# Top-k attention and an MLP: how many heads of a unit VectorE turns, and the order of the last batch

## The chip, the cores and the metric

The kernel runs on one core of a Trainium2 chip. The metric is the device time of one execution in microseconds (us). An execution uses five engines side by side: TensorE (PE in the profile; its weight loads are PEld), VectorE (DVE), ScalarE (ACT), GpSimd (POOL), and SyncE (SP), which here only issues DMAs. Each engine takes its instructions in the order in which the program was written, and waits for others by semaphores.

## The reference

Two blocks follow each other, in float32. Attention has 8 batches, 8 heads, 576 rows and 64 columns per head; of each row of scores only the 32 largest count:

```python
scores = scale * np.matmul(q, k.transpose(0, 1, 3, 2))
kth = np.partition(scores, -top_k, axis=-1)[..., -top_k:-top_k + 1]
scores = np.where(scores >= kth, scores, -1000000000.0)
attn = np.exp(scores - np.max(scores, axis=-1, keepdims=True))
attn = attn / (np.sum(attn, axis=-1, keepdims=True) + 1e-09)
x = np.matmul(attn, v)          # then (B,H,S,D) -> (B, S, H*D)
```

The MLP works on the rows of x (8 x 576 rows of 512):

```python
xn = (x - mu) / np.sqrt(var + 1e-06) * g_ln
out = x + np.maximum(xn @ w_ch1, 0.0) @ w_ch2     # 512 -> 2048 -> 512
```

The weights arrive as float64 and are converted on the chip, during the first batch.

## The kernel before, in words

**Units, groups and jobs.** The heads are taken in pairs, A and B. The 576 query rows of a pair are four tiles of 128 rows and a rest of 64. A *unit* is one tile for both heads (both heads' rests together fill one tile of 128). A *group* is some units of one head pair, a *job* has one group here. `parts` (L731 to L739) lists the groups of a batch: in batch 0 tiles 0 and 1, tiles 2 and 3, and the rest, each for all four head pairs; in batch 1 tiles 0 and 1, then 2, 3 and the rest; in batches 2 to 6 tiles 0, 1 and the rest, then 2 and 3. Batch 7 has the rest first, alone, for the four pairs, then tiles 0 and 1, then 2 and 3. That makes 160 units, 20 a batch.

**What a unit goes through.** `scores` (L329) multiplies on TensorE and copies to `sc` on ScalarE. `halve` (L363) and `select` (L381) find the 32nd largest score: VectorE takes maxima of eight and strikes them out (L391, L399, L386), GpSimd helps with two integer operations (L376, L379). `mask` and `weigh` on ScalarE (L426, L436) turn the scores into exponentials `e`, with their sums. Then `e` has to be turned, so that the keys lie on the partitions, as `pt`. There are two ways:

- `turn` (L481): TensorE transposes four blocks of 128 x 128 per head into PSUM (L490), and ScalarE copies them to `pt` (L502). A last block holds the last 64 keys of both heads (L519, L520); it always goes this way. Units of the rest always go this way too (L497, L510 to L513).
- `move` (L462): VectorE transposes 32 x 32 blocks within each head (L468, one instruction for a head), into the space of the unit's own scores; a DMA stores that to `turned` in device memory (L473) and four DMAs bring it back, each block to its partitions (L476). SP issues them.

`u.moved` (L763, L764) says which way: from batch 2 on, a unit is moved, with both heads, unless it is a rest or the last of its group. `values` (L539) then multiplies a group's `pt` with v on TensorE (L544, L551); `place` and `place_rest` turn the result back and scale it by the sums into `x`, the input of the MLP. The rest rows of two successive batches share one tile of x, `r`, so there is a rest tile for every second batch.

**Steps and the order written out by hand.** The loop from L894 runs over steps n. In step n VectorE selects unit n and halves unit n+1; TensorE makes the scores of unit n+2; unit n-1 is masked and unit n-2 weighed and turned or, at the step's end, moved; a group whose last unit is n-3 is multiplied with v. (The first units run one step closer.) All engines' instructions are written in this one order.

**The MLP as filling.** When the tiles of x of a job round are due, `give` (L847) adds a `Block` of them to the list `todo`: transposes of x (L648), hidden products (L664; 64 products, each as wide as the block has rows) and projections (L680; 16 products of 512 columns for each tile). Blocks have 2 tiles, or 3 with a rest tile (in batch 7: a block of 1, for the rest alone). The dictionary `gives` (L777 to L797) sets their steps. `fill` stands at eight places of a step and takes pieces off the list as long as their cost, in constants of the planner (0.44 a transposed tile, 0.0017 a row of a product), fits the pace that `slot` (L857) sets. Up to step 17 the pace is the difference of `dve_cost` and `pe_cost`; after it, `slot` divides what is left, less a reserve of 4.0, evenly over the steps to the next gifts, and takes the smallest such pace over all later gifts:

```python
for m in sorted(gives):
    if m > n:
        even = min(even, (left - RESERVE) / (m - n))
        left += sum(b.cost() for b in gives[m])
```

After the last gift (step 163) the whole list is taken without regard to VectorE. A tile of x is turned only a step after its rows were centred (`centred`, L622), and the list is taken strictly in order.

Of the kernel before, what the change touches and what calls it, by code (L numbers as in the profile page):

```python
# [21 lines left out]
J = 4  # L22
# [7 lines left out]
def kernel(  # L30
# [41 lines left out]
    nc = tc.nc  # L72
    P = nc.NUM_PARTITIONS
    B, H, S, D = q.shape
# [3 lines left out]
    JP = J * P  # L78
# [43 lines left out]
    def turned():  # L122
        return brief("tp")
# [18 lines left out]
    class Piece:  # L142
# [10 lines left out]
        def __init__(self, i):  # L153
            self.i = i
            if i < NF:
                self.c, self.nb = i % NC, i // NC
                n0 = self.nb * DM
                self.src = w_ch1[self.c * P : (self.c + 1) * P, 2 * n0 : 2 * (n0 + DM)]
                self.dst = w1[:, self.c, n0 : n0 + DM]
            else:  # L160
                f = i - NF
                self.src = w_ch2[f * P : (f + 1) * P, :]
                self.dst = w2[:, f, :]
# [146 lines left out]
    class Unit:  # L310
        def __init__(self, job, group, qt):
            self.job, self.group, self.qt = job, group, qt
            self.rest = qt == J
            self.tiles = [(0, 1)] if self.rest else [(0,), (1,)]

            self.moved = False
            self.e = None
            self.weighed = 0

# [130 lines left out]
    def place_of(u):  # L450

        g = u.group
        if g.pt is None:
            g.pt = ptpool.tile([P, 2 * J + 1, GQ], FP32, tag="pt", name="pt")
            g.blocks = g.pt[:, 0 : 2 * J].rearrange("p c n -> p (c n)").rearrange(
                "p (i h c n) -> p h i c n", h=2, c=J, n=32
            )
        return sum(P for x in g.qts if x < u.qt) // 32  # L460

    def move(u):  # L462

        i0 = place_of(u)
        ni = P // 32
        blocks = u.sc[:].rearrange("p t n -> p (t n)")[:, 0 : 2 * JP]
        for t in range(2):
            nc.vector.transpose(  # L468
                blocks.rearrange("p (j t c n) -> p j t c n", j=ni, t=2, c=J)[:, :, t],
                u.e[:, t, t * R : t * R + JP].rearrange("p (c j k) -> p j c k", c=J, k=32),  # L470
            )
        hbm = hbmpool.tile([P, 2 * JP], FP32, tag="turned", name="turned")
        nc.sync.dma_start(hbm[:], blocks)  # L473
        for j in range(ni):
            to = u.group.pt[j * 32 : (j + 1) * 32, 0 : 2 * J].rearrange("k c n -> k (c n)")
            nc.sync.dma_start(  # L476
                to[:, i0 * 2 * P : (i0 + ni) * 2 * P].rearrange("k (i x) -> k i x", i=ni),
                hbm[:, j * 2 * P : (j + 1) * 2 * P].rearrange("(i k) x -> k i x", k=32),
            )

    def turn(u):  # L481

        g = u.group
        i0 = place_of(u)
        q0 = i0 * 32

        def part(t):
            ps = turned()
            for c in range(J):
                nc.tensor.transpose(  # L490
                    ps[:, c * P : (c + 1) * P], u.e[:, t, c * P + t * R : (c + 1) * P + t * R],
                    ident[:],
                )
            if u.rest:
                both = ps[:].rearrange("p (c h n) -> p h c n", h=2, n=R)
                for h in range(2):
                    nc.scalar.copy(  # L497
                        g.blocks[:, h, i0 : i0 + R // 32],
                        both[:, h].rearrange("p c (i n) -> p i c n", n=32),
                    )  # L500
            else:
                nc.scalar.copy(  # L502
                    g.blocks[:, t, i0 : i0 + P // 32],
                    ps[:].rearrange("p (c i n) -> p i c n", c=J, n=32),
                )

        def last():
            ps = turned()
            if u.rest:
                nc.tensor.transpose(ps[0:R, 0:P], u.e[:, 0, JP:S], ident[:])  # L510
                nc.tensor.transpose(ps[:, P : 2 * P], u.e[:, 0, JP - R : S], ident[:])
                for h in range(2):
                    nc.scalar.copy(  # L513
                        g.pt[h * R : (h + 1) * R, 2 * J, q0 : q0 + R],
                        ps[h * R : (h + 1) * R, h * (P + R) : h * (P + R) + R],
                    )
            else:
                ends = u.e[:].rearrange("p t n -> p (t n)")[:, JP : JP + P]
                nc.tensor.transpose(ps[:, 0:P], ends, ident[:])  # L519
                nc.scalar.copy(g.pt[:, 2 * J, q0 : q0 + P], ps[:, 0:P])  # L520

        heads = () if u.moved else range(len(u.tiles))
        return [lambda t=t: part(t) for t in heads] + [last]

    xs, xps, rs, oTr, dr = {}, {}, {}, {}, {}
# [13 lines left out]
    def values(g):  # L539
        vb = g.job.v  # L540
        av = brief("av")
        for c in range(J):
            for h in range(2):
                nc.tensor.matmul(  # L544
                    av[h * D : (h + 1) * D, 0 : g.nq],
                    vb[:, h * J + c, :],
                    g.blocks[:, h, 0 : g.nq // 32, c, :],
                    start=(c == 0),
                    stop=False,
                )  # L550
        nc.tensor.matmul(  # L551
            av[:, 0 : g.nq], g.job.ends[:], g.pt[:, 2 * J, 0 : g.nq],
            start=False, stop=True,
        )
        g.oT = otpool.tile([P, GQ], FP32, tag="oT", name="oT")
        nc.scalar.copy(g.oT[:, 0 : g.nq], av[:, 0 : g.nq])  # L556
# [173 lines left out]
    for b in range(B):  # L730
        parts = [[0, 1], [2, 3], [J]]  # L731
        if b:
            parts = [[0, 1], [2, 3]]
            if b == B - 1:
                parts = [[J]] + parts
            else:
                parts[b < 2].append(J)
        for qts in parts:
            jobs += [Job(b, hp, [qts]) for hp in range(NHP)]  # L739
    units = []  # L740
# [20 lines left out]
    EARLY = jobs[NHP].first  # L761

    for u in units[jobs[5 * NHP].first :]:  # L763
        u.moved = not u.rest and u is not u.group.units[-1]  # L764


    full = slice(0, P)
# [9 lines left out]
    for j in jobs:  # L777
        if j.hp == NHP - 1:
            b = j.b
# [23 lines left out]
    def at(i):  # L803
        return units[i] if 0 <= i < N else None

    def after(n):

        turned = at(n - 1) if n - 1 < EARLY else at(n - 2) if n - 2 >= EARLY else None
        last = at(n - 2) if n - 2 < EARLY else at(n - 3) if n - 3 >= EARLY else None
        return turned, last.group if last and last is last.group.units[-1] else None  # L810

    def due(n):

        ahead = [n + 1] if n < CONVERTING else [n + 2]
        if n == CONVERTING:
            ahead = [n + 1, n + 2]
        return [units[i] for i in ahead if i < N]

    DVE_UNIT, DVE_REST, DVE_MOVE, DVE_TURN = 8.6, 5.0, 1.4, 1.45


    turns = {}
# [5 lines left out]
    def pe_cost(n):  # L828
        c = 0.0
        for x in due(n):  # L830
            c += 1.25 if x.rest else 1.5
        ex, g = after(n)
        if ex:
            c += 0.67 if ex.rest else 0.15 if ex.moved else 1.0
        if g:
            c += 0.6 + 7.8e-3 * g.nq
        return c

    def dve_cost(n):
        u, ex = at(n), after(n)[0]  # L840
        c = 4.0 if u is None else DVE_REST if u.rest else DVE_UNIT
        if n <= CONVERTING:
            c += 1.0
        c += DVE_TURN * (n in turns) + 0.85 * sum(b.n for b in gives.get(n, []))
        return c + DVE_MOVE if ex and ex.moved else c

    def give(n):  # L847
        early = not all(map(done, ready))
# [8 lines left out]
    def slot(n):  # L857


        if n <= CONVERTING:  # L860
            return max(0.0, dve_cost(n) - pe_cost(n)) / SLOTS
        left = sum(t[1] for t in todo)
        if n > last_give:
            even = left / max(1, END - 1 - n)
        else:
            even = 99.0
# [4 lines that stand above are left out]
        return max(0.0, even) / SLOTS  # L871
# [22 lines left out]
    for n in range(END):  # L894
# [4 lines left out]
        u, nxt, mk = at(n), at(n + 1), at(n - 1)  # L899
        ex, g = after(n)  # L900
# [3 lines left out]
        parts = turn(ex) if ex else []  # L904
# [1 line left out]
        last = ex and ex is ex.group.units[-1]  # L906
        quick = ex.group if last and ex.group.quick else None

        moved = ex is not None and ex.moved
        sent, stores[:] = stores[:], []  # L910

        if ex and not early:
# [21 lines left out]
        fill()  # L934
        if g:
            values(g)
        if parts and not moved:
            parts[0]()
        if ex and ex.rest:
            keep_den(ex)  # L940
# [58 lines left out]
        if moved:  # L999
            move(ex)  # L1000
# [46 lines left out]
```

## Time and profile before

Four executions took 1664.87 to 1668.89 us, with a median of 1666.33. The profiled one took 1668.89 us, its span from the first to the last instruction 1667.1 us, and the mean granted clock of TensorE was 0.981.

| | busy us | share of the span |
|---|---|---|
| TensorE | 1562.9 | 94% |
| TensorE's weight loads, beside it | 939.8 | 56% |
| VectorE | 1469.1 | 88% |
| ScalarE | 1041.7 | 62% |
| GpSimd | 672.3 | 40% |

Some groups of instructions: projection products L680 544.9 us, hidden products L664 552.0, VectorE's maxima L399 490.8 and strikes L386 391.9 and 125.9, its transposes in `move` L468 89.4 (136 of them), TensorE's transposes of e L490 96.5 (608), ScalarE's copies of them L502 69.8 (120).

In the lines of the profile an instruction group reads: line, engine, operation, what it writes and reads, shapes, count, busy us, mean ns of one, idle time of its engine just before, and who ended that idle time. A timeline row has the start, the length from there to the end of the merged instructions, engine, line, operation and count, and in brackets the idle time before it and who ended it. One float32 product appears as two records, one transpose as one. The ends of matmuls are modelled, so what a product costs is read from start to start.

### The profile page before, as it was taken

The page shows a single profiled execution, that of the slowest core. Times are in us where ns is not written, and L with a number is a line of the kernel's source. Part 1 is how long each engine was busy: PE and PEld are TensorE (multiplying, and loading weights), DVE is VectorE, ACT ScalarE, POOL GpSimd, SP SyncE. Part 2 cuts the span into 40 slices and gives each one's busy share as a digit, 9 for nine tenths or more (in the row PEclk, how much of TensorE's full clock was granted, in tenths as well). Part 3 has the DMA queues.
Part 4 walks back from the last instruction along what each step waited for, and adds up shares of the span by engine and source line. Part 5 has one row for each costly group of instructions (what it writes and reads, how often), then busy time and mean ns, then how long its engine had stood idle before and what let it go on. Part 6 is the DMA issues. An engine that isn't in the chain of part 4 may idle for free.

```text
span 1667.1 us, 24932 instructions
## 1 busy us (share of the span) xinstructions
PE 1562.9 (94%) x7057; PEld 939.8 (56%) x7057; DVE 1469.1 (88%) x4611; ACT 1041.7 (62%) x2615; POOL 672.3 (40%) x881
## 2 busy tenths in 40 slices
PE   2668899989899999999999999999999999999998
PEld 1336457556355475745547575745547575756764
DVE  5997999999999999999999999999879895988600
ACT  6886877767656666666656665656555565666620
POOL 5776763343443433343243433443243423333110
PEclk9878999999999999999999999999999999999999
DMA  7423333001433335233443335324333241222200
GB/s 176 88 81 92 95 62 61 22 14 22 100 107 88 99 82 135 91 91 89 108 120 95 86 103 127 97 71 99 99 96 99 72 114 48 60 78 69 81 13 13
DMA packets 303185, 139.30 MB, mean 84 GB/s; under 512 B 250820, under 2 KB 285640, under 8 KB 303048
## 3 DMA queue, kind: packets, MB, share of 16 engines
q1 hardware_dynamic: 298312, 137.12, 31.2%
q10 hardware_dynamic: 4736, 0.59, 0.3%
q8 instruction: 57, 0.93, 0.2%
q14 instruction: 80, 0.66, 0.1%
HBM read 92.54 MB, written 45.09 MB: 83 GB/s over the span
## 4 chain that ended last, share of the span: by engine, by line
PE 65%; DVE 23%; ACT 4%; issue 4%; POOL 3%; DMA 1%; SPq 0%; ACTq 0%; POOLq 0%; DVEq 0%
PE hps L664 23%; PE ops L680 22%; PE scps L354 7%; DVE m L399 7%; PE av L544 6%; DVE hi L386 6%; DVE hi L391 3%; DVE lo L386 2%; PE tp L490 2%; PE av L551 2%; DVE hi L375 2%; DVE size L193 1%; ACT sc L335 1%; POOL lo L376 1%; ACT e L426 1%
## 5 line engine op out<-in xcount | busy, mean ns | idle before, releaser
L664 PE MATMUL hps<-xT,w 128*128 128x256 f32 (+2 forms) x2176 | 552.0, 397 | 4.9 <-ACT xT L653 4.9
L680 PE MATMUL ops<-w,h 128*128 128x512 f32 x1152 | 544.9, 600 | 0.0
L399 DVE MAX8 m<-hi 128x8 f32<-128x304 f32 x1152 | 490.8, 464 | 3.3
L664 PEld LDWEIGHTS hps<-xT,w 128*128 128x128 f32 x2176 | 388.0, 191 | 110.0 <-issue 30.6
L376 POOL TENSOR_TENSOR lo<-sc,hi 128x576 int32<-128x576 int32 (+1 forms) x160 | 208.6, 1304 | 488.8 <-DVE hi L375 254.2
L386 DVE MATCH_REPLACE8 hi<-m,hi 128x304 f32<-128x304 f32 x864 | 391.9, 462 | 0.0
L680 PEld LDWEIGHTS ops<-w,h 128*128 128x128 f32 x1152 | 200.6, 191 | 185.9 <-issue 181.8
L391 DVE MAX8 hi<-lo 128x8 f32<-128x288 f32 x576 | 235.2, 446 | 38.3 <-POOL lo L379 37.2
L354 PE MATMUL scps<-kT,qT 64*128 64x288 f32 (+3 forms) x1344 | 222.1, 430 | 37.7 <-DVE qT L306 27.3
L335 ACT COPY sc<-scps 128x288 f32<-128x288 f32 x576 | 199.6, 408 | 70.2 <-PE scps L354 49.3
L426 ACT ACTIVATE e<-sc,m 128x576 f32<-128x576 f32 x288 | 224.1, 778 | 10.2 <-DVE m L399 7.1
L436 ACT ACTIVATE e<-e,bias 128x576 f32<-128x576 f32 x288 | 224.7, 780 | 0.7
L379 POOL TENSOR_TENSOR lo<-lo,sc 128x576 int32<-128x576 int32 (+1 forms) x160 | 207.2, 1295 | 12.5
L354 PEld LDWEIGHTS scps<-kT,qT 64*128 64x128 f32 (+1 forms) x1344 | 122.9, 179 | 154.0 <-issue 57.6
L544 PE MATMUL av<-pt,vb 128*64 128x256 f32 (+2 forms) x1152 | 148.3, 400 | 0.2 <-ACT pt L513 0.2
L675 ACT ACTIVATE h<-hps 128x512 f32<-128x512 f32 (+1 forms) x156 | 88.4, 567 | 87.1 <-PE hps L664 85.8
L375 DVE TENSOR_TENSOR hi<-sc 128x576 f32<-128x576 f32 (+1 forms) x160 | 115.3, 721 | 25.7 <-ACT sc L335 25.7
L386 DVE MATCH_REPLACE8 lo<-hi,lo 128x288 f32<-128x288 f32 x288 | 125.9, 445 | 0.0
L693 POOL TENSOR_TENSOR o<-o,x 128x512 f32<-128x512 f32 x32 | 42.0, 1313 | 207.3 <-ACT o L689 207.3
L556 ACT COPY oT<-av 128x256 f32<-128x256 f32 (+2 forms) x72 | 26.8, 373 | 157.7 <-PE av L551 157.7
L490 PE MATMUL tp<-ident,e 128*128 128x128 f32 x608 | 96.5, 283 | 27.9 <-ACT e L436 27.3
L544 PEld LDWEIGHTS av<-pt,vb 128*64 128x64 f32 x1152 | 75.9, 142 | 78.2 <-ACT e L436 15.1
(70 smaller groups left out, 1264.3 us busy)
## 6 DMA issues: line engine op xcount, KB each, us to landing
turned<-sc SPq DMA_DIRECT2D x68, 512.0 KB, 2.6
pt<-turned SPq DMA_DIRECT2D x272, 128.0 KB, 3.0
vb<-in_v_dram SPq DMA_DIRECT2D x144, 128.0 KB, 2.7
raw<-in_moe_w_ch_dram SPq DMA_DIRECT2D x32, 512.0 KB, 4.3
kin<-in_k_dram SPq DMA_DIRECT2D x128, 72.0 KB, 2.7
qin<-in_q_dram SPq DMA_DIRECT2D x120, 72.0 KB, 2.7
out_dram<-o SPq DMA_DIRECT2D x32, 256.0 KB, 2.1
ends<-in_v_dram SPq DMA_DIRECT2D x144, 16.0 KB, 2.3
```

Of the source, the lines that this page charges most:

```text
L335: nc.scalar.copy(u.sc[:, t, s * HALF : (s + 1) * HALF], made[s][t][:, 0:HALF])
L354: nc.tensor.matmul(ps[i * R : i * R + ql, o : o + width], qT[r, q0 : q0 + ql], kT[r, k0 : k0 + width], start=True, stop=True,)
L376: nc.gpsimd.tensor_tensor(lo.bitcast(I32), a.bitcast(I32), hi.bitcast(I32), ALU.subtract)
L379: nc.gpsimd.tensor_tensor(lo.bitcast(I32), lo.bitcast(I32), b.bitcast(I32), ALU.add)
L386: nc.vector.match_replace(x[:, t], m[:, t, :], x[:, t], LOWEST)
L391: nc.vector.max(u.hi[:, t, o : o + 8], u.lo[:, t])
L399: nc.vector.max(m[:, t, :], u.hi[:, t])
L426: nc.scalar.activation(u.e[:, t], u.sc[:, t], AF.Prelu, bias=u.thr[:, t, 7:8], scale=-1.0, alpha=SLOPE)
L436: nc.scalar.activation(u.e[:, t], u.e[:, t], AF.Exp, bias=u.bias[:, t : t + 1], scale=-scale / SLOPE, accum_out=g.den[:, col : col + 1],)
L544: nc.tensor.matmul(av[h * D : (h + 1) * D, 0 : g.nq], vb[:, h * J + c, :], g.blocks[:, h, 0 : g.nq // 32, c, :], start=(c == 0), stop=False,)
L664: nc.tensor.matmul(ps["h"][:, o : o + N], w1[:, c, f * P : (f + 1) * P], xT[0][:, c, 0:N], start=(c == 0), stop=(c == NC - 1),)
L680: nc.tensor.matmul(ps[i][:], hT[f][:, i * P : (i + 1) * P], w2[:, f, :], start=(f == 0), stop=(f == NF - 1),)
```

## The change

A unit's `moved` becomes a number of heads: 0, 1 or 2. From batch 2 to batch 4 the units that were moved with both heads have head B alone turned by VectorE and returned by DMA, and head A by TensorE and ScalarE; from batch 5 on they have both moved, as before. `move` works on the heads from `2 - nt` on and sends half as many bytes for one head. Batch 7 has the same groups as batches 2 to 6, so that its rest units come third in their groups, its rest tile goes into a block of three with tiles 0 and 1, and three of its five units of a head pair are moved rather than two. The planner's constants follow the number of heads.

```diff
-            self.moved = False
+            self.moved = 0
...
-        blocks = u.sc[:].rearrange("p t n -> p (t n)")[:, 0 : 2 * JP]
-        for t in range(2):
+        nt = u.moved
+        blocks = u.sc[:].rearrange("p t n -> p (t n)")[:, 0 : nt * JP]
+        for i, t in enumerate(range(2 - nt, 2)):
             nc.vector.transpose(
-                blocks.rearrange("p (j t c n) -> p j t c n", j=ni, t=2, c=J)[:, :, t],
+                blocks.rearrange("p (j t c n) -> p j t c n", j=ni, t=nt, c=J)[:, :, i],
                 u.e[:, t, t * R : t * R + JP].rearrange("p (c j k) -> p j c k", c=J, k=32),
             )
         hbm = hbmpool.tile([P, 2 * JP], FP32, tag="turned", name="turned")
-        nc.sync.dma_start(hbm[:], blocks)
+        nc.sync.dma_start(hbm[:, 0 : nt * JP], blocks)
         for j in range(ni):
             to = u.group.pt[j * 32 : (j + 1) * 32, 0 : 2 * J].rearrange("k c n -> k (c n)")
+            to = to.rearrange("k (i x) -> k i x", x=2 * P)[:, i0 : i0 + ni, (2 - nt) * P :]
             nc.sync.dma_start(
-                to[:, i0 * 2 * P : (i0 + ni) * 2 * P].rearrange("k (i x) -> k i x", i=ni),
-                hbm[:, j * 2 * P : (j + 1) * 2 * P].rearrange("(i k) x -> k i x", k=32),
+                to, hbm[:, j * nt * P : (j + 1) * nt * P].rearrange("(i k) x -> k i x", k=32)
             )
...
-        heads = () if u.moved else range(len(u.tiles))
+        heads = range(len(u.tiles) - u.moved)
...
-            if b == B - 1:
-                parts = [[J]] + parts
-            else:
-                parts[b < 2].append(J)
+            parts[b < 2].append(J)
...
-        u.moved = not u.rest and u is not u.group.units[-1]
+        if not u.rest and u is not u.group.units[-1]:
+            u.moved = 2 if u.job.b >= B - 3 else 1
...
-    DVE_UNIT, DVE_REST, DVE_MOVE, DVE_TURN = 8.6, 5.0, 1.4, 1.45
+    DVE_UNIT, DVE_REST, DVE_MOVE, DVE_TURN = 8.6, 5.0, 0.7, 1.45
...
-            c += 0.67 if ex.rest else 0.15 if ex.moved else 1.0
+            c += 0.67 if ex.rest else 1.0 - 0.44 * ex.moved
...
-        return c + DVE_MOVE if ex and ex.moved else c
+        return c + DVE_MOVE * ex.moved if ex else c
...
-        moved = ex is not None and ex.moved
+        moved = ex is not None and ex.moved > 0
...
-        if parts and not moved:
+        if len(parts) > 1:
             parts[0]()
```

## The prediction

> **What bounds the kernel now.** I read the page's busy lines and slices first, then the busy time by batch, then single rows of TensorE's timeline to see whether a busy TensorE is a working one.
>
> ```profile
> PE 1562.9 (94%) x7057; PEld 939.8 (56%) x7057; DVE 1469.1 (88%) x4611; ACT 1041.7 (62%) x2615; POOL 672.3 (40%) x881
> PE   2668899989899999999999999999999999999998
> DVE  5997999999999999999999999999879895988600
> ```
>
> TensorE (PE) is idle mainly in the first ten slices, where batches 0 and 1 run and the weights are converted; VectorE (DVE) is full from there to slice 28, then has gaps. Who ends last has to be read by batch. The halving on VectorE runs once per unit; its 41st, 61st, 81st, 101st, 121st and 141st starts, at 408.7, 592.7, 777.0, 962.6, 1149.8 and 1357.7 us, cut the span into batches 2 to 7. Busy time of the engines in these stretches:
>
> ```profile
> 408.70:592.70 184.00, 175.97 (x717) 90.89 (x714) 181.19 (x569) 114.70 (x301) 73.92 (x105) 0.98 0.36 92
> 592.70:777.00 184.30, 182.12 (x825) 110.43 (x824) 182.81 (x579) 117.64 (x305) 71.41 (x102) 1.00 0.38 102
> 777.00:962.60 185.60, 185.60 (x796) 103.80 (x797) 182.66 (x573) 117.39 (x302) 70.91 (x98) 1.00 0.37 100
> 962.60:1149.80 187.20, 185.52 (x848) 113.71 (x845) 184.37 (x579) 119.22 (x309) 74.66 (x105) 1.00 0.37 101
> 1149.80:1357.70 207.90, 206.90 (x892) 122.39 (x890) 184.46 (x575) 120.55 (x307) 71.31 (x101) 1.00 0.35 93
> 1357.70:1570.00 212.30, 210.41 (x1095) 138.65 (x1094) 181.09 (x582) 129.41 (x329) 73.70 (x107) 1.00 0.26 70
> ```
>
> After the stretch's length come PE, PEld, DVE, ACT and POOL busy. PE is idle for 8.0, 2.2, 0, 1.7, 1.0 and 1.9 us in batches 2 to 7; VectorE is within 3 us of the length up to batch 5 and far below it in 6 and 7. Both are nearly full in 2 to 5; the later batches are PE's alone. Is a busy PE at its own speed? Rows of its timeline and of the chain that ended last:
>
> ```profile
> 1011.20 0.60 PE L490 MATMUL tp<-ident,e 128*128 128x128 f32 x4
> 1011.64 0.59 PE L680 MATMUL ops<-w,h 128*128 128x512 f32 x1
> ...
> 1019.33 2.37 PE L544 MATMUL av<-pt,vb 128*64 128x320 f32 x16
> 1022.28 1.02 PE L680 MATMUL ops<-w,h 128*128 128x512 f32 x2
> ...
> 1412.93 0.69 PE L544 MATMUL av<-pt,vb 128*64 128x64 f32 x16
> 1413.82 0.61 PE L490 MATMUL tp<-ident,e 128*128 128x128 f32 x4
> ...
> 1454.48 1.95 PE L544 MATMUL av<-pt,vb 128*64 128x256 f32 x16
> 1456.89 1.02 PE L680 MATMUL ops<-w,h 128*128 128x512 f32 x2
> ```
>
> ```profile
> 761.91 1.94 PE hps L664 x6
> 1499.34 2.01 PE hps L664 x18
> 1548.80 2.59 PE hps L664 x12
> 1597.18 7.73 PE ops L680 x18
> ```
>
> From start to start, four transposes take 0.44 us (1011.20 to 1011.64), the value products of one group 2.95, 0.89 and 2.41 us at 320, 64 and 256 queries, and one record of the MLP 0.323 us at 384 rows, 0.112 at 128, 0.216 at 256 and 0.429 in the projection (each product has two records). The projection runs at the same 0.429 in the tail, where VectorE is done, and in the middle. So a busy PE is at full speed from batch 2 on: **PE's sum of work sets the end**, and VectorE matters only where PE waits.
>
> The Trainium skill, Perfetto Trace Analysis, section Identifying the Most-Contended Engine, says that matmul busy time misjudges TensorE and that weight-load occupancy should be used, with plain occupancy for VectorE. By it TensorE would have headroom (56%) and VectorE (88%) be the bound; batches 2 to 4 would then each lose VectorE's 7.9 us and batch 7 gain 5.3, some 18 us off, 1648 us. The start-to-start times above speak against it here: a product of 512 rows occupies TensorE for 0.43 us while its weight load is busy for 0.19.
>
> **The change part by part.** The rows for what moves, and the one large wait:
>
> ```profile
> L468 DVE STREAM_TRANSPOSE sc<-e 128x512 f32<-128x512 f32 x136 | 89.4, 688 | 25.8 <-ACT e L436 25.6
> L490 PE MATMUL tp<-ident,e 128*128 128x128 f32 x608 | 96.5, 283 | 27.9 <-ACT e L436 27.3
> 458.61 1.12 PE L648 MATMUL tp<-ident,r 128*128 128x128 f32 x4 [5.29 <-POOL r L619]
> ```
>
> (a) Head A in batches 2 to 4. Twelve units a batch are turned by VectorE; 36 heads go back to PE: 36 x 0.44 = **+15.8 us** on the path. VectorE loses 36 x 0.657 (89.4/136) = 23.7 us, which shortens nothing where PE has no gap. PE's gaps in these batches are 8.0 and 2.2 us. The largest is 5.3 us: PE has no more MLP work until the rest rows of batches 0 and 1 are centred, after VectorE's statistics. Two moves come before it in VectorE's order (the first transposes start at 436.7), so the rows come 1.3 us earlier and PE 0.9 us later: 2.2 recovered. Of the small ones (0.5 to 1.0 us each, behind ScalarE copies) I take 0.5, of the 2.0 us in batch 3, where hidden products wait for ScalarE's copy of the turned rows, 1.0. **-3.7**, bounds 0 and -10.2.
>
> (b) Batch 7. 12 of its units move instead of 8: 8 heads fewer on PE, -3.5. The value products of a lone rest group and of 256 queries become one of 320: 4 x (0.89 + 2.41 - 2.95) = -1.4. Hidden products of 128 and 256 rows become 384: 64 x 2 x (0.112 + 0.216 - 0.323) = -0.6. **-5.5 us** on the path. VectorE gains 8 x 0.657 = 5.3 us, beside PE's work: it stands at 181 of 212 us there, and if PE did not cover it, that is the 5.3 at stake.
>
> (c) The pace of the MLP work. slot() spreads what is left evenly up to the tightest later gift. Blocks of 3, 2 and 1 tiles cost 85.4, 56.9 and 34.3 by the planner's constants. At step 116 (end of batch 5) 4.4 + 85.4 lie ready. Before, the tightest is step 143: (89.8 + 2 x 56.9 - 4)/27 = 7.4 a step, about 7.4 to the end. After, the lone rest block at 148 is gone and step 156 rules: (89.8 + 3 x 56.9 - 4)/40 = 6.4, and from 156 on (3.5 + 85.4 - 4)/7 = 12.1. Some 40 us move from steps 116 to 155 into the last seven. The work stays; it costs only where PE runs dry. The planner's units are worth 0.98 us (0.858/0.8755). Batch 5: PE 185.5 - 4 x 0.98 = 181.6 against VectorE's 184.4, 2.8 short, covered by the lead that VectorE gains in (a). Batch 6: 206.9 - 20 x 0.98 = 187.3 against 184.5, covered. First 16 steps of batch 7: PE's own part of batch 6 is 207 - 145 = 62 us, 3.1 a step, so 16 x (6.3 + 3.1) = 150 us, against VectorE's at most 16/20 of 186. Step 156 repeats the end of a planner period with only 3.5 left, where PE may wait for the rest rows as at 458.6; the same place in batch 4, near 754 us, cost 2.0. VectorE is ahead there: I take **+0.5** for (c), bounds -4.6 (the gaps of batches 5 to 7 vanish) and +8.1 (2.8 without the lead, and 5.3).
>
> (d) At nothing. ScalarE copies 28 more heads, 28 x 0.58 = 16 us, beside work: 118 of 184 us become 125 of 190 in a batch; on PE's side each new part needs its head's exponentials, in the step in which unmoved units need theirs; that wait sums to 27.3 us in 13 cases, nearly all before 408 us. If this cover is gone, see the stalls below. SP issues 72 moves with 288 returns for 68 and 272, 36 of them half as large, in pieces of 512 B for 1 KB, and 16 loads of v fewer. A move lands in 2.6 and 3.0 us; one issued at 1007.2 is read at 1019.3. Half or double that time fits into 12.1 us, so the stores and loads behind it on SP see little. No wait is added to an engine that was not there for unmoved units.
>
> Sum: 15.8 - 3.7 - 5.5 + 0.5 = **+7.1 us**. The profiled execution took 1668.9 us (span 1667.1), 2.6 above the median; on the median it gives 1673.4. With the bounds: 15.8 - 10.2 - 5.5 - 4.6 = -4.5 (1661.8) to 15.8 - 5.5 + 8.1 = +18.4 (1684.7).
>
> **Rivals.** *PE's gaps close* (the other side): a lighter VectorE lets PE run without a gap from 408 us. Each us recovered beyond the 10.3 us of net work (15.8 - 5.5) is a gain; all 14.8 us give 1661.8. For it: VectorE is at 98 to 99% where the gaps are. Against: most are behind ScalarE or the order of the gifts, and only two moves precede the largest.
> *PE starves in batches 5 to 7*: at 6.4 a step VectorE's 184 us a batch rule, and the late three-tile block makes PE wait at step 156: +18.4, 1684. For it: in batches 3 to 5 the same pace stood even with VectorE. Against: VectorE starts with a lead.
> *The new parts stall PE*: if 12 of the 36 wait like the 13 earlier cases, 2.1 us each, +25 more, 1698. Against: the four-packs after 550 us run at 0.44.
> *The change does little*: VectorE is the true bound, and PE's added work fits into gaps: in batches 2 to 4, -24 + 5.3 in batch 7, 1648. Against: PE's rows leave no gaps.
>
> **How the numbers follow.** What a measurement can tell from no change is 0.2%, 3.3 us: 1663.0 to 1669.7. Forecast 0.62, its own range 1668 to 1679, of which 0.10 lies within 0.2%; closing gaps 0.15 (0.07 faster, 0.08 same); starving 0.13 and stalls 0.05, slower; VectorE the bound 0.05, faster. Faster 0.12, same 0.18, slower 0.70. The range 1662 to 1684 reaches from the closed gaps to starving and leaves out stalls, VectorE and the edges, below 0.2.
>
> **What would show it.** L490 x720 and L468 x108; no products of 128 rows at L664. By the halving's starts: batch 2 some 186.5 us, 3 188.5, 4 191; batch 5 186, 6 188; PE busy near 1573 us and full from batch 2 on. VectorE near 174 us in batches 2 to 4. Steps 156 to 162 take some 105 us. I am wrong if batches 2 to 4 don't grow by a PE part of 5 us each, if PE shows gaps over 3 us in batches 5 to 7, or if new waits of L490 for L436 appear.

## The result

The changed kernel takes 1671.29 us (median) against 1667.43 us for the kernel before: a ratio of 1.0020 with a 95% interval of 1.0015 to 1.0026, that is 3.4 us slower (2.5 to 4.3; the two medians lie 3.9 us apart). The forecast was 7.1 us slower. The direction and the bound were right; about half of the size was not there.

The page of the changed kernel, busy lines and slices (line numbers from `move` on are one or more higher than before):

```profile
PE 1573.1 (94%) x6969; PEld 933.1 (56%) x6969; DVE 1451.8 (87%) x4583; ACT 1058.1 (63%) x2643; POOL 673.2 (40%) x879
...
PE   2669999989899999999999999999999999999998
...
DVE  5997999999999998999898999999999999997000
```

TensorE's busy time rose by 10.2 us over the whole span (1562.9 to 1573.1), but 0.9 of it lies ahead of batch 2, which the change does not touch. From batch 2 on it rose by 9.3 us (1238.4 to 1247.7), where the prediction's work came to 15.8 - 5.5 = 10.3. VectorE is lighter in the slices of batches 3 and 4 and now full up to slice 36. The busy time by batch, cut at the same starts of the halving (the first part, up to batch 2, happened to be 2.6 us shorter in this execution, so lengths are compared from 406.1 us here and 408.7 us before):

```profile
406.10:590.90 184.80, 179.06 (x751) 94.51 (x749) 174.06 (x558) 119.56 (x307) 73.73 (x105) 0.98 0.25 62
590.90:778.80 187.90, 187.35 (x881) 115.89 (x878) 176.15 (x567) 124.38 (x317) 71.80 (x102) 1.00 0.27 67
778.80:968.10 189.30, 189.30 (x838) 108.07 (x837) 175.51 (x561) 123.56 (x312) 69.66 (x98) 1.00 0.26 65
968.10:1157.60 189.50, 188.34 (x860) 115.27 (x858) 182.82 (x579) 122.31 (x314) 74.09 (x105) 1.00 0.35 95
1157.60:1344.00 186.40, 185.77 (x791) 103.12 (x790) 182.84 (x573) 117.04 (x300) 71.00 (x98) 1.00 0.37 99
1344.00:1667.60 323.60, 317.88 (x1284) 190.34 (x1283) 191.06 (x599) 147.85 (x368) 83.61 (x118) 1.00 0.22 65
```

Before, the same stretches were 184.0, 184.3, 185.6, 187.2, 207.9 and 309.4 us long. Batches 2 to 4 grew by 8.1 us together, although VectorE works 7 us less in each (174 to 176 for 181 to 183): they are TensorE's. Batch 6 lost 21.5 us and the end gained 14.2: the later MLP work. The stretches from batch 5 on lost 5.0 us; the sum is 3.1 us above before.

These cuts are starts on VectorE, and a lighter VectorE runs further ahead of TensorE, so they divide TensorE's time unevenly: in the split of the heads alone (below), batch 5, whose work is the same as before, is 3.3 us longer by them (190.5 for 187.2). Cut instead at TensorE's own scores of the third unit of each batch, batches 2 to 4 grew by 2.8, 3.0 and 5.2 us, 11.0 together, and what follows lost 8.0. Batch 4 by these cuts, before and changed:

```profile
785.70:970.60 184.90, 184.90 (x801) 105.32 (x800) 181.54 (x569) 117.39 (x301) 72.95 (x101) 1.00 0.38 102
...
788.90:979.00 190.10, 190.10 (x849) 110.16 (x848) 173.49 (x556) 123.92 (x313) 70.60 (x101) 1.00 0.26 66
```

TensorE is never idle in either. It makes 48 transposes more, those of 12 heads, and the stretch is 5.2 us longer, although VectorE works 8 us less in it.

What TensorE waited for from 400 to 760 us of the changed kernel, that is in batch 2 and nearly all of batch 3 (engine and line, releaser, us in total, times, longest; batch 4 has no idle time in either kernel):

```profile
PE tp L649 <- POOL r L620: 5.3, 1, 5.3
PE scps L354 <- ACT x L561: 0.3, 1, 0.3
PE scps L354 <- ACT xT L654: 0.3, 1, 0.3
```

The same stretch before:

```profile
PE tp L648 <- POOL r L619: 5.3, 1, 5.3
PE hps L664 <- ACT xT L653: 2.0, 1, 2.0
PE xo L583 <- ACT oT L556: 1.0, 2, 0.5
PE scps L354 <- ACT xT L653: 1.0, 1, 1.0
PE tp L519 <- ACT e L436: 0.7, 1, 0.7
```

10.0 us of gaps became 6.1 (with one of 0.2 us at 760.7, just behind the stretch of this list). From 1150 to 1640 us the changed kernel shows

```profile
PE xo L584 <- ACT oT L557: 0.9, 2, 0.5
PE hps L665 <- ACT xT L654: 0.2, 1, 0.2
```

where the kernel before had

```profile
PE tp L648 <- ACT sc L335: 2.2, 3, 1.0
PE tp L490 <- ACT e L436: 0.4, 1, 0.4
PE tp L648 <- POOL less L616: 0.3, 1, 0.3
```

No new wait of the transposes L491 for the exponentials L436 appears after batch 2 began, though there are 112 transposes more.

### The profile page after: what moved, and what is told of

The parts are those of the page before. It is cut to its first block, busy times and chain, and to the rows that moved or that the text cites. A ratio compares the mean times of both kernels' runs of the same rounds, so it can differ in the third digit from the quotient of the medians.

```text
span 1667.6 us, 24789 instructions
## 1 busy us (share of the span) xinstructions
PE 1573.1 (94%) x6969; PEld 933.1 (56%) x6969; DVE 1451.8 (87%) x4583; ACT 1058.1 (63%) x2643; POOL 673.2 (40%) x879
## 4 chain that ended last, share of the span: by engine, by line
PE 69%; DVE 19%; issue 4%; ACT 3%; POOL 3%; DMA 1%; ACTq 0%; POOLq 0%; DVEq 0%
PE hps L665 25%; PE ops L681 24%; PE scps L354 8%; PE av L545 6%; DVE m L399 6%; DVE hi L386 5%; DVE hi L391 3%; PE tp L491 3%; PE av L552 2%; DVE lo L386 2%; DVE hi L375 1%; DVE size L193 1%; PE tp L649 1%; POOL lo L376 1%; POOL lo L379 1%
## 5 line engine op out<-in xcount | busy, mean ns | idle before, releaser
L665 PE MATMUL hps<-xT,w 128*128 128x256 f32 (+1 forms) x2048 | 551.6, 412 | 2.3 <-ACT xT L654 2.3
L665 PEld LDWEIGHTS hps<-xT,w 128*128 128x128 f32 x2048 | 371.3, 191 | 116.4 <-issue 29.7
L436 ACT ACTIVATE e<-e,bias 128x576 f32<-128x576 f32 x288 | 224.9, 781 | 0.7
L491 PE MATMUL tp<-ident,e 128*128 128x128 f32 x720 | 113.6, 282 | 26.0 <-ACT e L436 25.4
L491 PEld LDWEIGHTS tp<-ident,e 128*128 128x128 f32 x720 | 91.4, 146 | 80.3 <-ACT e L436 36.0
```

Of the source, the lines that this page charges most:

```text
L436: nc.scalar.activation(u.e[:, t], u.e[:, t], AF.Exp, bias=u.bias[:, t : t + 1], scale=-scale / SLOPE, accum_out=g.den[:, col : col + 1],)
L491: nc.tensor.transpose(ps[:, c * P : (c + 1) * P], u.e[:, t, c * P + t * R : (c + 1) * P + t * R], ident[:],)
L665: nc.tensor.matmul(ps["h"][:, o : o + N], w1[:, c, f * P : (f + 1) * P], xT[0][:, c, 0:N], start=(c == 0), stop=(c == NC - 1),)
```

## The experiments

All were timed in five rounds against the kernel before on the same chip. In the expectations, theory P is the prediction's: TensorE's sum of work sets the end and VectorE counts only through TensorE's gaps; rival V says that VectorE bounds batches 2 to 5; rival S that TensorE starves at the slower pace.

**The order of batch 7 alone.** Both heads stay moved from batch 2 on:

```diff
-            u.moved = 2 if u.job.b >= B - 3 else 1
+            u.moved = 2
```

> Batch 7 in the groups of batches 2 to 6, VectorE turning both heads of every moved unit from batch 2 on. Theory P (TensorE's sum of work sets the end, VectorE counts only through TensorE's small gaps): 5.5 us of work leave TensorE and the gaps stay as they are, so 5 us below the kernel before (3 to 7); TensorE busy near 1557 us. Rival S (with the slower pace of the MLP work in batches 5 to 7 VectorE rules there and TensorE starves): not below the kernel before, 0 to 8 us above it, with gaps of TensorE of 3 us and more in batches 5 to 7. Rival V (VectorE is the true bound in batches 2 to 5): within 2 us of the kernel before or above it, for VectorE has 5 us more to do in batch 7.

Measured: 1659.06 against 1667.75 us, ratio 0.9944 (0.9932 to 0.9956), 9.3 us faster (7.3 to 11.3). The second half of the change, alone, makes a faster kernel. It gave more than theory P said, and nothing of S or V is seen. Its stretches from batch 5 on:

```profile
960.80:1146.90 186.10, 184.94 (x846) 113.52 (x842) 183.73 (x579) 120.04 (x311) 74.64 (x105) 1.00 0.37 101
1146.90:1333.40 186.50, 185.87 (x794) 103.18 (x792) 182.92 (x574) 116.96 (x300) 70.82 (x98) 1.00 0.37 100
1333.40:1656.90 323.50, 317.81 (x1284) 190.27 (x1283) 191.00 (x599) 147.84 (x368) 83.37 (x118) 1.00 0.22 65
```

TensorE is idle for 1.2 and 0.6 us in batches 5 and 6, although VectorE gained no lead in batches 2 to 4: 182.9 us of VectorE's work and 185.9 of TensorE's fit into 186.5 us side by side. The two engines nearly balance there, and neither starves the other. Gaps between TensorE's instructions from batch 5 to the end of VectorE's work sum to 2.2 us, against 4.5 before. In batch 2, where the order changes nothing, TensorE was idle for 1.0 us less than before; that is chance, for in the five kernels of this document with the same work there it was idle for 7.0 to 8.4 us.

**The split of the heads alone.** Batch 7 as in the kernel before:

```diff
-            parts[b < 2].append(J)
+            if b == B - 1:
+                parts = [[J]] + parts
+            else:
+                parts[b < 2].append(J)
```

> Head A back on TensorE and ScalarE in batches 2 to 4, batch 7 with the rest first as before. Theory P: 15.8 us of work come to TensorE and some 7 us of its gaps close, so 9 us above the kernel before (7 to 12); TensorE busy near 1579 us. Rival V: VectorE loses 23.7 us in the batches that it bounds, so at or below the kernel before (-10 to +2). The sum of this run's difference and that of the order alone should give the 3.4 us of the whole change if the two parts don't work on each other.

Measured: 1679.06 against 1667.75 us, ratio 1.0067 (1.0054 to 1.0079), 11.2 us slower (9.0 to 13.2). The prediction had 15.8 - 3.7 = 12.1 for it. Rival V, at or below the kernel before, falls. With the order's -9.3 the sum is +1.9, with some 3 us of uncertainty, against the 3.4 of both at once: the parts add up as far as this can tell.

**VectorE relieved, nothing put on TensorE.**

```diff
         for t in range(2):
+            if t == 0 and u.job.b < B - 3:
+                continue
             nc.vector.transpose(
```

> The kernel before without VectorE's transposes of head A in batches 2 to 4 (36 instructions left out, nothing in their place; the DMAs carry the scores that lie there, so head A's weights are wrong in these batches). Theory P: TensorE's work is the same, only its gaps shorten: 3 to 7 us below the kernel before. Rival V: 15 us or more of the 23.7 us that VectorE loses.

Measured: 1665.26 against 1667.75 us, ratio 0.9986 (0.9977 to 0.9994), 2.3 us faster (1.0 to 3.8). The page shows 17.9 us less on VectorE than before:

```profile
PE 1566.4 (94%) x7057; PEld 941.7 (57%) x7057; DVE 1451.2 (87%) x4575; ACT 1042.5 (63%) x2615; POOL 670.2 (40%) x881
```

By the mean of a transposition 23.7 us of work were left out; little came of it. TensorE's gaps between the start of batch 2 and the end of VectorE's work fell from 14.5 to 11.6 us.

**More relief.** Both heads' transposes left out:

```diff
         for t in range(2):
+            if u.job.b < B - 3:
+                continue
             nc.vector.transpose(
```

> The kernel before without any of VectorE's transposes of e in batches 2 to 4 (72 instructions, 47 us left out, nothing in their place; both heads' weights are wrong there). The first relief, of 36, gave 2.3 us. Theory P: what VectorE's delay costs TensorE is nearly used up, so 2 to 5 us below the kernel before. Rival V: each transposition left out is worth the same, so 5 us or more, growing with the dose.

Measured: 1663.77 against 1667.17 us, ratio 0.9978 (0.9969 to 0.9986), 3.7 us faster (2.3 to 5.2) for 47 us less on VectorE. The second dose of 36 is worth 1.4 us by the medians of the two runs' ratios, and some 4 us at the widest. TensorE's gaps, 11.5 us, are those of the first relief (11.6): the second dose closed none. VectorE's work in batches 2 to 4 has almost no price.

**Work added to TensorE, VectorE not relieved.**

```diff
         if parts and not moved:
             parts[0]()
+        elif moved and ex.job.b < B - 3:
+            ps = turned()
+            for c in range(J):
+                nc.tensor.transpose(
+                    ps[:, c * P : (c + 1) * P], ex.e[:, 0, c * P : (c + 1) * P], ident[:]
+                )
```

> The kernel before with four more transposes of head A on TensorE, read by nobody, in each of the 36 moved units of batches 2 to 4; VectorE and ScalarE do what they did. Theory P: 15.8 us of work more, of which the gaps of batch 2 take what lies before its 460 us (under 2 us): 13 to 16 us above the kernel before. Rival V: TensorE has room where VectorE rules, so 0 to 6 us above it.

Measured: 1680.00 against 1667.75 us, ratio 1.0071 (1.0057 to 1.0084), 11.8 us slower (9.5 to 14.0). The median lies below the 13 to 16 that were expected, the interval reaches into them. Of 15.8 us of work, 2.8 went into gaps by the trace (14.5 to 11.7 us between batch 2 and the end of VectorE's work): more than the 2 us that I had allowed, since the gap of 2.0 us in batch 3 closed too, by added work alone. The price of head A on TensorE is thus the same, within some 3 us, with and without VectorE's relief (11.2 and 11.8).

**The pace alone.** Groups and moves of the kernel before, the MLP work later:

```diff
+        if 116 <= n < 156:
+            even = min(even, 6.4)
         return max(0.0, even) / SLOTS
```

> The kernel before, groups and moves untouched, with the pace of the MLP work held at 6.4 at most in steps 116 to 155 (it was 7.4), so that the work comes later as in the changed kernel. Theory P: the sum of TensorE's work is the same and VectorE keeps up, so within 2 us of the kernel before. Rival S (at that pace VectorE rules): 5 us above it or more, with new gaps of TensorE between batch 5 and step 156.

Measured: 1665.65 against 1667.17 us, ratio 0.9989 (0.9980 to 0.9998), 1.8 us faster (0.3 to 3.3). The later work costs nothing and even gains a little. TensorE's waits in this run from 1150 to 1640 us:

```profile
PE xo L583 <- ACT oT L556: 1.0, 2, 0.5
```

The three waits of the turned rows of x for ScalarE's score copies (2.2 us in the kernel before) are gone, as they are in the changed kernel. Rival S falls: TensorE is asked for less, VectorE works 183.9 us of a batch 6 that is now 188.2 us long (207.9 before), and no new gap opens.

**The split kept for a batch more**, in the changed kernel:

```diff
-            u.moved = 2 if u.job.b >= B - 3 else 1
+            u.moved = 2 if u.job.b >= B - 2 else 1
```

> The changed kernel with the split kept through batch 5 (head B alone on VectorE in batches 2 to 5, both from batch 6). Theory P: 12 more heads of 0.44 us come to TensorE, 5.2 us, and there is hardly a gap left to close in batch 5 (1.2 us in the changed kernel): 4 to 5.2 us above the changed kernel, 7.5 to 9 above the kernel before. Rival V: another 7.9 us leave VectorE, so no slower than the changed kernel, 3.4 above the kernel before or less.

Measured: 1673.77 against 1666.16 us, ratio 1.0043 (1.0030 to 1.0056), 7.2 us slower than the kernel before (5.0 to 9.3), 3.8 above the changed kernel by the ratios. The expected 7.5 to 9 lie in the interval, though its middle is a little lower. Twelve more heads cost again about what twelve cost before.

**The first two moved units of batch 2 on TensorE**, on top of the order of batch 7 alone:

```diff
-            u.moved = 2 if u.job.b >= B - 3 else 1
+            u.moved = 2 if u.i >= jobs[5 * NHP].first + 2 else 0
```

> The order of batch 7 alone (9.3 us below the kernel before), and the first two moved units of batch 2 left to TensorE entirely. Theory P with a refinement (up to some 455 us VectorE sets the pace and TensorE has gaps): VectorE reaches the rest rows' statistics 2.6 us earlier and 1.8 us of new work of TensorE fall into gaps, so 2 us below the order alone: 9 to 13 below the kernel before. Plain sum of TensorE's work: 1.8 us above the order alone, 7.5 below the kernel before.

Measured: 1659.99 against 1667.17 us, ratio 0.9955 (0.9942 to 0.9967), 7.5 us faster (5.5 to 9.7): the plain sum's number, and the median of my refinement missed, though runs of this size can't tell 7.5 from 9.3. The wait for the rest rows did end 1.8 us earlier from the start of batch 2 (48.0 for 49.8 us), so the gate moved as expected, but the end did not follow: from the start of batch 2 the span is 1250.5 us, against 1249.8 for the order alone. TensorE's gaps are 1.0 us shorter and its busy time 1.6 us longer.

**VectorE's idle end used.** On top of the order of batch 7 alone, the last units of batch 7's last four groups moved too:

```diff
-        if not u.rest and u is not u.group.units[-1]:
-            u.moved = 2 if u.job.b >= B - 3 else 1
+        if not u.rest and (u is not u.group.units[-1] or u.i >= N - 7):
+            u.moved = 2
```

> The order of batch 7 alone, and the last units of batch 7's last four groups turned by VectorE too, which is idle beside TensorE there. Theory P: 8 heads of 0.44 us leave TensorE, 3.5 us below the order alone: 11 to 14 below the kernel before. Rival W (the round trip through memory, 2.6 and 3.0 us, comes too late for the value products that follow in the next step): TensorE waits up to 3 us in each of the four groups, so not below the order alone, 9 us or less below the kernel before.

Measured: 1657.71 against 1667.17 us, ratio 0.9937 (0.9924 to 0.9949), 10.5 us faster (8.5 to 12.7); not told apart from the order alone. From the start of batch 2 its span is 1.7 us shorter (1248.1 for 1249.8) rather than 3.5, and the timelines of VectorE, SP and TensorE show where 1.6 us went:

```profile
1483.43 1.29 DVE L469 STREAM_TRANSPOSE sc<-e 128x512 f32<-128x512 f32 x2
...
1484.74 0.34 SPq L474 DMA_DIRECT2D turned<-sc  x1
1487.43 1.74 SPq L478 DMA_DIRECT2D pt<-turned  x4
1489.21 0.43 SPq L292 DMA_DIRECT2D vb<-in_v_dram  x1
...
1489.65 1.04 PE L649 MATMUL tp<-ident,x 128*128 128x128 f32 x8
1492.28 1.95 PE L545 MATMUL av<-pt,vb 128*64 128x256 f32 x16 [1.59 <-DMA vb<-in_v_dram]
```

The move is issued at 1484.74, and its four returns from 1487.43 to 1489.17; the value products start at 1492.28. The row names the load of v, which came last on the queue. But by the landing times in the trace that load landed at 1492.4, 3.2 us after its issue at 1489.21 and after the products had begun; the last of the four returns, issued at 1488.74, landed at 1491.9. So the wait was for the moved unit's return. Then the same with the last three groups only (`N - 5`):

> As the run with the last units of batch 7's last four groups turned by VectorE, but only those of the last three groups: the first one's round trip made TensorE wait 1.6 us in a step in which the list of MLP work was held up. Theory P: 6 heads of 0.44 us leave TensorE, 2.6 us, and no new gap comes: 1 us better than with all four, some 12 us below the kernel before (10 to 13), below that of the order alone. Rival W: the wait of 1.6 us moves to the next group, so no better than with all four.

Measured: 1657.19 against 1666.16 us, ratio 0.9945 (0.9932 to 0.9959), 9.2 us faster (6.8 to 11.3). The gap is gone from the trace and no other came from batch 5 on, yet from the start of batch 2 the spans are 1247.9 us here, 1248.1 with all four groups and 1249.8 for the order alone. The 2.6 us expected are 1.9 by the spans (batch 2, which is the same work in all three, had 1.4 us more of gaps here than in the order alone) and nothing that the timing can tell. So three kernels lie 9 to 10.5 us below the kernel before, and further below the changed one: the order alone, and these two, which can't be ranked.

## Why the prediction was right in kind and off in size

**What bounds the kernel: right.** TensorE's work from batch 2 on went up by 9.3 us, of 10.3 that were worked out, and the kernel got slower with VectorE 17 us lighter. Work added to TensorE costs its length less a few gaps (11.8 of 15.8 us); work taken from VectorE gives 2.3 and 3.7 us for 24 and 47. Reading a record from start to start showed this ahead of the run; the occupancies (94% and 88%, and 56% for the weight loads) did not. Here the Trainium skill, Perfetto Trace Analysis, section Identifying the Most-Contended Engine, warns of matmul busy time and names two measures in its place, the share of TensorE's peak rate that the products reach and weight-load occupancy. The second, 56% beside VectorE's 88%, would have named VectorE, and the two reliefs speak against that; the first was not worked out here.

**(a) Head A: right.** +15.8 of work and -3.7 of gaps gave 12.1; the split alone measured 11.2 (9.0 to 13.2). The gaps of batches 2 to 4 fell from 10.0 to 6.1 us, 3.9. The sum held, but not the place, and so far it was luck. I had 2.2 us recovered from the wait for the rest rows, and that wait stayed at 5.3 us: its end moved 1.3 us nearer to the start of batch 2, as worked out (49.9 to 48.7 us), but TensorE's last work before it moved by as much. The scores ahead of this wait were themselves held, by ScalarE's copy of the turned rows (before, then changed):

```profile
452.08 1.24 PE L354 MATMUL scps<-kT,qT 64*128 64x288 f32 x4 [0.96 <-ACT xT L653]
...
448.22 1.24 PE L354 MATMUL scps<-kT,qT 64*128 64x288 f32 x4 [0.29 <-ACT xT L654]
454.75 1.12 PE L649 MATMUL tp<-ident,r 128*128 128x128 f32 x4 [5.29 <-POOL r L620]
```

The wait ends 6.53 us after their start in both kernels, and so it does in the first relief, where nothing was added to TensorE and the wait is 5.3 us as well. What ties the two together was not tested. The smaller gaps, of which I took 1.5 us, gave all of the 3.9.

**(b) Batch 7's work: consistent.** -5.5 us was counted from rows. The order alone measured -9.3 (7.3 to 11.3); from the start of batch 2 its span is 8.6 us shorter, of which gaps account for 3.3 (14.5 to 11.2 us; 1.0 of it is the chance in batch 2) and 5.3 remain for the work.

**(c) The pace: the step that failed.** It was taken as +0.5 us between -4.6 and +8.1, because I feared a starving TensorE more than I trusted gaps to close. Measured: -1.8 us (0.3 to 3.3) with the pace alone, and gaps of batches 5 to 7 that fall from 4.5 to 2.2 us in the changed kernel, -2.3. The row that I had not weighed stood in the trace of before: the waits of the turned rows of x for ScalarE's score copies, 2.2 us, came at the faster pace only and left with it: they stand in all five traces at that pace and in none of the seven at the slower one. The lead of VectorE, which I had used as cover in batch 5, was not even needed: without it (the order alone) TensorE was idle for 1.2 us there.

With the gaps as measured the sum is 15.8 - 3.9 - 5.5 - 2.3 = 4.1 us, against 3.1 by the spans from batch 2 on and 3.4 (2.5 to 4.3) by the runs; the 1.0 us between 4.1 and 3.1 is TensorE's work, 9.3 for 10.3. The 2.8 us by which (c) was off are most of the difference from 7.1; the rest lies within what the runs can tell.

**(d) Nothing: right.** The DMAs of the changed kernel (KB each, us to landing):

```profile
turned<-sc SPq DMA_DIRECT2D x36, 512.0 KB, 2.6
pt<-turned SPq DMA_DIRECT2D x144, 128.0 KB, 3.0
...
turned<-sc SPq DMA_DIRECT2D x36, 256.0 KB, 2.0
pt<-turned SPq DMA_DIRECT2D x144, 64.0 KB, 2.0
```

The single-head moves land sooner (4.0 for 5.6 us together), although in pieces half as long. ScalarE's 28 more copies raised its busy time by 16.4 us, unseen in the time.

Of the rivals, TensorE's gaps did close further than forecast, by part of the 14.8 us that were at stake and not beyond the 10.3 at which the sign turns. Starving, stalls of the new parts and a bounding VectorE each met a run that spoke against it.

**The sign of being wrong.** The prediction called itself wrong if batches 2 to 4 did not grow by 5 us of TensorE's work each. By its own cuts they grew by 0.8, 3.6 and 3.7 us, so to the letter this sign spoke against it. By TensorE's cuts batch 4, which had no gap to lose, grew by 5.2; batches 2 and 3, where gaps of 2.3 and 1.6 us closed, by 2.8 and 3.0. The work was there; the cuts, and a sign that left out the prediction's own -3.7, were the fault. The two other signs, gaps over 3 us in batches 5 to 7 and new waits for the exponentials, did not show.

## What to carry to other kernels

When two engines are both near full, read the busier one's instructions from start to start at the same shape, in a stretch where it is surely alone and in the disputed one; equal spacing means that it works at its own speed, and then its sum of work can be added up: here it came out at 15.9 us for 15.8 (the split alone), 5.3 for 5.5 (the order alone) and 9.3 for 10.3 (both). Test a mixed change by its halves: here one half made the kernel 11 us slower and the other 9 us faster, and together they looked like almost nothing. Gaps that are there before a change deserve the same tally as work, each with what ends it and what the change does to that.

## What was not expected

Two engines that each need 183 to 186 us in a batch of 186.5 us ran side by side with 0.6 us of idle time on TensorE (batch 6 of the order alone): so fine an interleaving, in an order fixed beforehand, lost almost nothing to waiting. And of four moves whose values follow in the very next step, only the first made TensorE wait, 1.6 us; it fell into the step after which the rest tile of x is centred, with little MLP work on the list. Whether that is why was not tried.
